# A chunked linear-attention scan with a list scheduler: decays scanned in place, smaller holdings for v and y's decays, other numbers of buffers, and an offset per kind of step

## The chip, the cores and the metric

One core of a Trainium2 chip. The metric is the device time of the whole kernel in microseconds, median over runs. PE is TensorE (PEld its weight loads), DVE VectorE, ACT ScalarE, POOL GpSimd, SP the engine that issues nearly all DMAs.

## The reference

A recurrence over 768 tokens for 4 batches of 8 heads with a 40x40 state each, and then a mixture of 8 experts over the 3072 rows that come out.

```python
for t in range(S):
    y[:, :, t] = np.einsum('bhd,bhde->bhe', rt, state)
    Sa = np.einsum('bhde,bhe->bhd', state, at)
    state_decay = state * wt[:, :, None, :] - np.einsum('bhd,bhe->bhde', Sa, bt)
    state = state_decay + np.einsum('bhd,bhe->bhde', vt, kt)
...
logits = x @ w_gate
expert_idx = np.argmax(logits, axis=1)
...
h = np.maximum(np.einsum('ecd,edf->ecf', disp, w1), 0.0)
y = np.einsum('ecf,efd->ecd', h, w2)
```

Each token goes to one expert, up to a capacity of 768, and is scaled by its softmax gate.

## The kernel before

**Tiling of the scan.** The four batches form two pairs (`pr`), two batches side by side on the 128 partitions. The tokens go in six blocks (`i`) of 128, each of two chunks (`c`) of 64. A block of a pair is numbered n = 2i + pr. The work of one n:

- `decay` (lines 349 to 372): two loads of w, one for products forward from the middle of a group, one backward. DVE scans them (`forth`, `back`) against the tile `seed`, which holds a one at the start of each group, into E and K, the halves of tile R. There are two R, one for each pair. `over`, `divide` and `ends` bring them to one reference point and give the decay of whole chunks, `wf`.
- `prep`: kb (b and k) and a are multiplied by K and E (lines 426, 430). On PE, `xt` (447) forms the 64x64 token products of a chunk in the PSUM tile pd. `take_k` masks one part into an X tile, `xt_inv` (469 and a helper) copies the other into `xd` and `x21`. `kt` and `et` (475) transpose kb into `bk` and E into `EE`, and four DMAs bring `EE` into a tile E, which `take_y` reads.
- `inverse`, once in a block for both pairs and both chunks: the inverse of the unit triangular 32x32 parts, in all partitions at once. `begin` (542) transposes `xd` on DVE, `elim` (556, 558) makes 31 steps of a product and a sum, 62 instructions, each of which reads the one before, `back_a` and `back_b` (563, 567) transpose back. `diag` and `comb` (587) put 64x64 inverses together in the tiles `nt`, by PE and ACT.
- `chain`, for each chunk in order, because it carries the state ST: `enter` (636) decays it, `state` (641) transposes it, `zz` (657, 661) multiplies X by u and the state by a, `take_z` (674) adds the two, `sa` (685) applies `nt`, `turn_sa` and `take_sa` put the result beside v in the tile u, `snew` (720) and `take_snew` (728, 730) give the next state. `out`: `qpm` (739), a mask, `ymm` (754, 760), `take_y` (772). `gate`: y as two fp16 parts, transposed by a DMA, and stored; the router's logits (841).

After each block, `route` counts the tokens of each expert on DVE and PE, and four scatters on POOL's queue (1094) write the block's list. The last block's stretch also holds `prefetch` (the first expert's weights, through the tile `wt`, which is one of the two w tiles) and `first_expert`. The expert stage, from a second scheduler with buffers of its own, follows.

A mask (`masked`, line 56 on) has two forms. On DVE it is one product with the tile `mask` (67). Otherwise ACT copies the tile and POOL clears half of it with two affine selects (61, 64).

**What sets the order.** `steps(name)` collects steps with durations by engine, e.g. `"V.71|A.6 G1.4"` for a mask: DVE, or ACT and then POOL. `order` is a list scheduler: it repeatedly takes, of all steps whose `needs` are given and whose `take` buffers are free, the one with the lowest start plus `later[name] + mu * plan - o_tail * tail`, where `plan` is a due time. Of a step's forms it takes the one with the least end plus `PRICE` times the engine's time. The instructions are then issued in that order, each engine working through its own in order. A step that frees a buffer gives it to the next in line. `BUFS` gives the number of buffers of each name: four X, four `nt` (a block needs four of each, one for each pair and chunk), four `bk`, one `xd`, `x21`, `xu` and `nu`. `LATER` is empty, so `later` is 0 for all steps.

```python
LATER = {}
BUFS = {"pd": 2, "ps": 4, "w": 2, "a": 4, "r": 2, "sv": 3, "sat": 2, "u": 3, "bk": 4, "E": 3, "EE": 1, "X": 4, "nt": 4, "zv": 2,
...
able.append((t + plus, index[name], name, t, plus))
```

`load` issues the DMAs of kb, a, r, vt (into `sv`) and v (into u, both chunks of an n in one tile).

Of the kernel before, what the change touches and what calls it, by code (L numbers as in the profile page):

```python
# [22 lines left out]
class Schedule:  # L23
# [69 lines left out]
    def order(self, mu):  # L93
# [26 lines left out]
        later = {x: self.later.get(x.rstrip("0123456789"), 0.0) for x in threads}  # L120
# [98 lines left out]
def scan_part(ctx, tc, two, w, kb, a, r, vt, v, wg, xd, lg, ident, up, SX, slot2, route, prefetch, fill, early):  # L219
# [26 lines left out]
    SHAPE = {"w": ([P, H * P], F32), "a": ([P, H, P], F32), "r": ([P, 2, H // 2, P], F32), "sv": ([P, 2, H // 2, 2, C], F32),  # L246
             "sat": ([P, H // 2, 2, C], F32),
             "u": ([P, 2, 2, HD], F32), "bk": ([P, 2, HD], F32), "E": ([P, 2, HD], F32), "EE": ([P, 2, HD], F32), "zv": ([P, HD], F32), "X": ([P, H * C], F32),
# [17 lines left out]
    wt = free_["w"][0]  # L266
# [10 lines left out]
    seed = one.tile([P, NG * C], F32, name="seed")  # L277
# [55 lines left out]
    def decay(T):  # L333
# [40 lines left out]
        for z in range(2):  # L374
            steps(f"load_w{pr}")(lambda z=z: start(z), "L0>1.5", take=["w"], gives=("load_w", n, z))
        add = steps(f"decay{pr}")
        add(forth, "V2.3", needs=[("load_w", n, 0)] + [("R", n - NR)] * (n >= NR), free=["w"])
        add(back, "V2.3", needs=[("load_w", n, 1)])
        add(over, "V.6", free=["w"])
# [4 lines left out]
    def load(T):  # L384
# [9 lines left out]
        def fetch(name, x):  # L394
            y = T[name] = get(name)
            if name == "u":

                for z in range(2):
                    dma(y[half(z), :, 1 - z], x[pr, i, half(z)].rearrange("p (c n) -> p c n", c=2))
            else:  # L400
                dma(y.rearrange("p h t -> p (h t)") if name == "a" else y.rearrange("p x j t -> p (x j t)"), x[pr, i])
# [15 lines left out]
    def prep(T, G):  # L417
# [1158 lines left out]
```

## Time and profile before

| | |
|---|---|
| median of 3 runs | 825.42 us (825.19 to 826.05) |
| profiled execution, its own time | 818.57 us |
| its span on the core | 816.8 us |
| mean granted PE clock | 0.798 |
| busy PE, PEld | 590.3 us (72%), 468.9 us (57%) |
| busy DVE, ACT, POOL | 496.6 us (61%), 284.8 us (35%), 226.8 us (28%) |

The span runs from the first instruction to the last. Busy times of different engines overlap. The clock is that of PE in shares of 2.4 GHz. An engine's share over the whole span mixes the scan with the expert stage, so the rows below give windows as well.

### The profile page before, as it was taken

Reading aid. Unit: us, or ns where it says so; the run is one execution under the profiler, and the core shown is the slowest. Engines: PE = TensorE matmul, PEld = TensorE weight load, DVE = VectorE, ACT = ScalarE, POOL = GpSimd, SP = SyncE. Lnnn points to the kernel's source line nnn. Section 1 sums busy time; section 2 is a strip of 40 time slices with the busy share of each in tenths; the row PEclk is TensorE's granted clock in tenths of the full one; section 3 lists DMA queues with packets and bytes.
Section 4 is the critical chain, followed back from the end, with each engine's and each line's share of the span. In section 5 each row is a group of like instructions: output and inputs, shape, how many; then the busy total and the mean of one; then the engine's idle time right before and its main releaser. Section 6 shows DMA issues by size and latency. Waiting matters only on the chain. (4 is left out here: it accounts for less than half of the span.)

```text
span 816.8 us, 23980 instructions
## 1 busy us (share of the span) xinstructions
PE 590.3 (72%) x10388; PEld 468.9 (57%) x10388; DVE 496.6 (61%) x979; ACT 284.8 (35%) x615; POOL 226.8 (28%) x302
## 2 busy tenths in 40 slices
PE   0524978287828874797579739968897789799991
PEld 0414868287717764796578639854473445445651
DVE  5899878963996699769973794426331353252320
ACT  0313433352406331534154425424422344143320
POOL 4201342131302431243123202422353143243110
PEclk9975667576965987588659965789998899899996
DMA  8922573356623664455433325476749674665200
GB/s 297 334 69 60 164 229 115 101 103 115 224 98 89 121 213 140 76 116 174 145 71 71 93 82 106 86 158 180 199 75 231 145 162 144 176 167 155 65 10 19
DMA packets 105970, 109.78 MB, mean 134 GB/s; under 512 B 70360, under 2 KB 88282, under 8 KB 105856
## 3 DMA queue, kind: packets, MB, share of 16 engines
q1 hardware_dynamic: 97856, 92.67, 44.2%
q0 software_dynamic: 4256, 9.99, 4.2%
q10 hardware_dynamic: 3744, 5.51, 2.5%
q8 instruction: 83, 1.36, 0.7%
q14 instruction: 31, 0.25, 0.1%
HBM read 83.60 MB, written 10.94 MB: 116 GB/s over the span
## 5 line engine op out<-in xcount | busy, mean ns | idle before, releaser
L1261 PE MATMUL ps<-w,hh 128*128 128x320 f16 (+1 forms) x672 | 101.5, 311 | 15.7 <-ACT hh L1395 12.5
L1398 DVE SCALAR_TENSOR_TENSOR hh<-ps,hh 128x480 f16<-128x480 f32 (+2 forms) x72 | 37.3, 559 | 111.8 <-ACT hh L1395 111.8
L1261 PEld LDWEIGHTS <-hh 128*128 128x128 f16 (+1 forms) x696 | 71.8, 106 | 47.6 <-ACT hh L1395 14.5
L587 PE MATMUL ps<-nu,x 32*32 32x32 f32 x768 | 21.7, 236 | 99.6 <-DVE nu L567 99.6
L1388 PE MATMUL ps<-xT,w 128*128 128x480 f16 (+1 forms) x448 | 84.8, 352 | 5.3 <-DMA xT<-xt 5.3
L587 PEld LDWEIGHTS ps<-nu,x 32*32 32x32 f32 x768 | 21.1, 151 | 100.8 <-ACT nt L56 56.7
L1388 PEld LDWEIGHTS <-w 128*128 128x128 f16 (+1 forms) x512 | 43.4, 98 | 59.3 <-issue 20.5
L556 DVE TENSOR_TENSOR xd<-xu,nu 128x31 f32<-128x31 f32 (+15 forms) x186 | 70.4, 378 | 6.5
L558 DVE TENSOR_TENSOR nu<-nu,xd 128x31 f32<-128x31 f32 (+15 forms) x186 | 70.3, 378 | 6.4
L739 PE MATMUL pd<-r,sv 64*128 64x64 f32 x768 | 65.1, 335 | 8.2 <-DVE xd L469 8.2
L739 PEld LDWEIGHTS pd<-r,sv 64*128 64x128 f32 x768 | 61.6, 242 | 11.7 <-DVE xd L469 9.7
L1181 DVE SCALAR_TENSOR_TENSOR w<-s,w 128x640 f16<-128x640 f32 (+1 forms) x49 | 47.0, 992 | 32.2 <-ACT w L1180 32.2
L754 PE MATMUL ps<-bk,qp 128*64 128x64 f32 (+1 forms) x768 | 57.9, 256 | 9.2 <-POOL qp L64 9.2
L1265 POOL DMA_INDIRECT out_dram<-ob,ri x26 | 25.8, 991 | 130.1 <-ACT ob L1414 111.3
L636 POOL TENSOR_TENSOR ST<-ST,wf 128x320 f32<-128x320 f32 x17 | 14.9, 886 | 155.8 <-DVE ST L730 109.8
L760 PE MATMUL ps<-S,r 128*64 128x64 f32 (+1 forms) x704 | 54.7, 257 | 3.5 <-issue 3.5
L1180 ACT ACTIVATE w<-s 128x640 f16<-128x640 f32 (+1 forms) x49 | 40.5, 876 | 43.9 <-DMA s<-in_moe_w_dram 43.7
L754 PEld LDWEIGHTS ps<-bk,qp 128*64 128x64 f32 x768 | 47.1, 168 | 12.0 <-POOL qp L64 10.1
L1094 POOL DMA_INDIRECT meta<-mt,sloti x24 | 27.5, 1145 | 78.6 <-DVE mt L1091 73.2
L760 PEld LDWEIGHTS ps<-S,r 128*64 128x64 f32 x704 | 45.6, 171 | 3.9 <-issue 3.9
L1395 ACT ACTIVATE hh<-ps 128x480 f16<-128x480 f32 (+2 forms) x72 | 31.7, 494 | 38.1 <-PE ps L1388 25.0
L64 POOL TENSOR_SCALAR_AFFINE_SELECT qp<-qp 64x512 f32<-64x512 f32 x42 | 28.4, 677 | 53.9 <-ACT qp L61 45.1
(182 smaller groups left out, 1220.4 us busy)
## 6 DMA issues: line engine op xcount, KB each, us to landing
w<-in_w_dram SPq DMA_DIRECT2D x24, 512.0 KB, 5.1
slot<-in_kb_dram SPq DMA_DIRECT2D x24, 512.0 KB, 5.6
sv<-in_vt_dram SPq DMA_DIRECT2D x24, 512.0 KB, 3.3
s<-in_moe_w_dram SPq DMA_DIRECT2D x14, 512.0 KB, 5.0
a<-in_a_dram SPq DMA_DIRECT2D x12, 512.0 KB, 6.4
r<-in_r_dram SPq DMA_DIRECT2D x12, 512.0 KB, 3.8
s<-in_moe_w_dram SPq DMA_DIRECT2D x16, 320.0 KB, 5.3
xd<-x SPq DMA_DIRECT2D x24, 192.0 KB, 3.2
```

The lines of the kernel that those rows point to most:

```text
L556: return (lambda: nc.vector.tensor_mul(tv, xu[:, s + 1:, s:s + 1].to_broadcast([P, n, m]), nu[:, s:s + 1, 0:m].to_broadcast([P, n, m])), l ...
L558: lambda: nc.vector.tensor_add(o, o, tv))
L587: nc.tensor.matmul(pa[o, u * 32:(u + 1) * 32], x21[f, uu, :], (n1 if which == 0 else ntd)[f, uu, :], start=True, stop=True)
L739: nc.tensor.matmul(pp[:, h % 2, cols(4 * x + j, C)], T["sv", c][f, x, j].rearrange("p z t -> p (z t)"), T["r"][f, x, j, tok], start=True, ...
L754: nc.tensor.matmul(py[half(x), into(h)], R["qp"][:, h % 2, 4 * x + h // 2, :], T["bk"][c][:, x, wide(h)], start=True, stop=q == 0)
L760: nc.tensor.matmul(py[half(x), into(h)], T["r"][:, x, h // 2, tok], S_[:, lo:lo + (C if h < H - 1 else D)], start=False, stop=True)
L1180: return (lambda: nc.scalar.activation(h, s(), AF.Copy, scale=SW), lambda: nc.vector.scalar_tensor_tensor(l, s(), SW, h, ALU.mult, ALU.sub ...
L1181: lambda: nc.vector.scalar_tensor_tensor(l, s(), SW, h, ALU.mult, ALU.subtract))
L1261: nc.tensor.matmul(po[:, :DM], h[l], rr[:, f, :], start=(f == 0 and m == 0), stop=(f == NF - 1 and m == 2))
L1388: nc.tensor.matmul(s_["h", f + z][:, :n], l, rr, start=m % 7 == 0 and m < 14, stop=m >= 14)
L1395: nc.scalar.activation(s_["hh"][:, 0, f, :n], s_["h", f][:, :n], AF.Relu)
L1398: nc.vector.scalar_tensor_tensor(s_["hh"][:, 1, f, :n], s_["h", f][:, :n], 0.0, s_["hh"][:, 0, f, :n], ALU.max, ALU.subtract)
```

## The change

1. w is loaded into R, and the scans work in place; `over` then stands between the two scans, since it reads w of the backward half (as K) before `back` overwrites it. A load of w waits for R, that is for the muls and `et` of n - 2. The two w tiles are gone; `wt` is a tile of its own, and `seed` is fp16.
2. u and E hold one chunk each: five half-size tiles in place of three whole ones. v is loaded chunk by chunk; a chunk's tile is freed at `snew` (u) or `take_y` (E).
3. Numbers of buffers: X 4 to 7, `nt` 4 to 6, `bk` 4 to 5, `sv` 3 to 2, `zs` 4 to 3.
4. `LATER` holds an offset for each kind of step (a step's name without its digits); `MU` and `PRICE` change. `divide` is always on DVE.

```diff
-    MU = 0.003
-    O_TAIL = 0.0
+    MU = 0.0016
+    O_TAIL = 0
...
-    PRICE = {"V": 1.5, "A": 0.4, "G": 0.2}
+    PRICE = {"V": 3.41, "A": 1.41, "G": 0.14}
...
-    LATER = {}
+    LATER = {"R": 2.12, "chain": 0.019, "comb": -0.079, "decay": 0.178, "diag": -0.044, "early": 2.414,
...
-    BUFS = {"pd": 2, "ps": 4, "w": 2, "a": 4, "r": 2, "sv": 3, "sat": 2, "u": 3, "bk": 4, "E": 3, "EE": 1, "X": 4, "nt": 4, "zv": 2,
-            "xd": 1, "x21": 1, "xu": 1, "nu": 1, "zs": 4, "S": 2, "qp": 2, "y": 2, "x16": 3, "xT": 2}
+    BUFS = {"pd": 2, "ps": 4, "a": 4, "r": 2, "sv": 2, "sat": 2, "u": 5, "bk": 5, "E": 5, "EE": 1, "X": 7, "nt": 6, "zv": 2,
+            "xd": 1, "x21": 1, "xu": 1, "nu": 1, "zs": 3, "S": 2, "qp": 2, "y": 2, "x16": 3, "xT": 2}
...
-    wt = free_["w"][0]
+    wt = two.tile([P, H * P], F32, name="wt")
...
-    seed = one.tile([P, NG * C], F32, name="seed")
+    seed = one.tile([P, NG * C], F16, name="seed")
...
         def forth():
-            nc.vector.tensor_tensor_scan(E, s_[0], seed, 0.0, ALU.mult, ALU.add)
-            put("w", s_[0])
+            nc.vector.tensor_tensor_scan(E, E, seed, 0.0, ALU.mult, ALU.add)
+
+        def over():
+
+            nc.vector.tensor_mul(se[pr], Eg[:, :, M - 1::M], Kg[:, :, M - 2::M])
+            nc.vector.reciprocal(si[pr], se[pr])
 
         def back():
-            nc.vector.tensor_tensor_scan(K[:, ::-1], s_[1][:, ::-1], seed, 0.0, ALU.mult, ALU.add)
...
+            nc.vector.tensor_tensor_scan(K[:, ::-1], K[:, ::-1], seed, 0.0, ALU.mult, ALU.add)
...
+        for z, x in enumerate((E, K)):
+            steps(f"load_w{pr}{z}")(lambda z=z, x=x: dma(x, w[z, pr, i]), "L0>1.5",
+                                    needs=[("R", n - NR)] * (n >= NR), gives=("load_w", n, z))
...
+        def fetch_u(c):
+
+            y = T["u", c] = get("u")
+            for z in range(2):
+                dma(y[half(z), 1 - z], v[pr, i, half(z), c * HD:(c + 1) * HD])
...
-            y = T["E"] = get("E")
-            for x in range(2):
-                for c in range(2):
-                    dma(y[half(x), c, :], T["EE"][half(c), x, :])
+            for c in range(2):
+                y = T["E", c] = get("E")
+                for x in range(2):
+                    dma(y[half(x)], T["EE"][half(c), x, :])
```

The order of the instructions changes on all engines. Two places show it. Line numbers of the changed kernel are two to four above those of before.

DVE, the third elimination (block 2) at its end, in the kernel before; all 62 rows of 556 and 558 stand in this manner, and the chain's `take_snew` (730), `take_y` (772) and `take_z` (674) of block 1 follow:

```order
L556 TENSOR_TENSOR xd_152<-xu_154,nu_155 128x60
L558 TENSOR_TENSOR nu_155<-nu_155,xd_152 128x2x30
L556 TENSOR_TENSOR xd_152<-xu_154,nu_155 128x31
L558 TENSOR_TENSOR nu_155<-nu_155,xd_152 128x31
L563 STREAM_TRANSPOSE xu_154<-nu_155 128x32x32
L567 STREAM_TRANSPOSE nu_155<-xu_154 128x1024
L730 TENSOR_TENSOR ST_208<-ps_115,ST_209 128x8x40
L772 SCALAR_TENSOR_TENSOR y_164<-ps_117,E_140 128x320
L772 SCALAR_TENSOR_TENSOR y_165<-ps_114,E_138 128x320
L674 TENSOR_TENSOR zs_158<-pd_112,zv_150 128x320
```

In the changed kernel the same elimination (560, 562), some rows before its end, with `take_z` (678), a mask of qp (70) and `take_snew` (733) of block 1 in it:

```order
L560 TENSOR_TENSOR xd_159<-xu_161,nu_162 128x252
L562 TENSOR_TENSOR nu_162<-nu_162,xd_159 128x18x14
L678 TENSOR_TENSOR zs_165<-pd_112,zv_158 128x320
L560 TENSOR_TENSOR xd_159<-xu_161,nu_162 128x255
L562 TENSOR_TENSOR nu_162<-nu_162,xd_159 128x17x15
L560 TENSOR_TENSOR xd_159<-xu_161,nu_162 128x256
L562 TENSOR_TENSOR nu_162<-nu_162,xd_159 128x16x16
L70 TENSOR_TENSOR qp_168<-pd_113,mask 128x512
L560 TENSOR_TENSOR xd_159<-xu_161,nu_162 128x255
L733 TENSOR_TENSOR ST_213<-ps_116,ST_214 128x8x40
L562 TENSOR_TENSOR nu_162<-nu_162,xd_159 128x15x17
L560 TENSOR_TENSOR xd_159<-xu_161,nu_162 128x252
```

What stood behind the 62 rows, and more of the chain that had stood ahead of them, now stands between them; `take_y` rows (775) also stand further up and down.

POOL, in the kernel before, around the four scatters of a block's list (1094), in block 2's part of the program; `enter` (636) and two differences of the gate (824, 825) follow them:

```order
L548 AFFINE_SELECT nu_155<-nu_155 128x1024
L1094 DMA meta_70<-mt,sloti 6144x4
L1094 DMA meta_71<-mt,sloti 6144x4
L1094 DMA meta_72<-mt,sloti 6144x4
L1094 DMA meta_73<-mt,sloti 6144x4
L636 TENSOR_TENSOR ST_207<-ST_207,wf 128x8x40
L636 TENSOR_TENSOR ST_209<-ST_209,wf 128x8x40
L824 TENSOR_TENSOR x_0_166<-y_164,x_0_166 128x320
L825 TENSOR_TENSOR x_0_166<-y_164,x_0_166 128x64
```

In the changed kernel, with what each waits for (DMASW are the semaphores of POOL's own DMAs, here of the scatters; line 67 is a mask's affine select, 640 `enter`):

```order
L640 TENSOR_TENSOR ST_214<-ST_214,wf 128x8x40 [waits DVE_49,Pool_49]
L67 AFFINE_SELECT X_146<-X_146 64x512 [waits Activation_49]
L67 AFFINE_SELECT X_146<-X_146 64x512 [waits Pool_49]
L1096 DMA meta_70<-mt,sloti 6144x4 [waits DVE_49,Pool_49]
L1096 DMA meta_71<-mt,sloti 6144x4
L1096 DMA meta_72<-mt,sloti 6144x4
L67 AFFINE_SELECT qp_168<-qp_168 64x512 [waits Activation_49]
L67 AFFINE_SELECT qp_168<-qp_168 64x512 [waits DMASW6_49,DMASW5_49,DMASW4_49]
L67 AFFINE_SELECT qp_168<-qp_168 64x512 [waits Activation_49]
L67 AFFINE_SELECT qp_168<-qp_168 64x512
L67 AFFINE_SELECT qp_169<-qp_169 64x512 [waits Activation_49]
L67 AFFINE_SELECT qp_169<-qp_169 64x512
```

Three of the four scatters now stand directly ahead of the qp masks, whose second select waits until those three have landed, and masks of X and qp that were DVE's (67 before) are on POOL.

## Rows read from the trace of the kernel before

**Rows 1.** The instructions of line 542 (`begin`): count, durations in ns, first and last start.

```profile
L542 DVE STREAM_TRANSPOSE xu<-xd x6: 1943/1966/1980, 43.9 to 458.3; 128x1024 f32<-128x1024 f32 x6
```

**Rows 2.** Windows over periods: length, busy us (instructions) by engine, PEclk, DMA share, GB/s.

```profile
43.90:126.20 82.30, 46.51 (x1138) 41.88 (x1138) 69.18 (x126) 28.97 (x67) 21.86 (x16) 0.65 0.44 133
...
126.20:458.30 332.10, 240.22 (x6116) 224.05 (x6116) 252.72 (x535) 122.64 (x292) 86.15 (x103) 0.73 0.48 122
...
298.60:380.70 82.10, 60.80 (x1530) 56.86 (x1530) 67.05 (x138) 31.43 (x75) 23.48 (x27) 0.73 0.50 127
...
458.30:546.90 88.60, 66.03 (x1418) 60.85 (x1419) 52.96 (x123) 33.32 (x75) 24.53 (x39) 0.69 0.45 108
```

**Rows 3.** Windows over parts of periods: start, two eliminations, a second part, the expert stage.

```profile
0.00:43.90 43.90, 12.75 (x296) 10.77 (x296) 31.54 (x40) 9.20 (x17) 13.76 (x40) 1.00 0.86 294
...
43.90:72.60 28.70, 3.08 (x72) 2.80 (x72) 26.40 (x67) 2.87 (x8) 0.00 (x0) 0.60 0.15 48
...
298.60:330.00 31.40, 16.94 (x308) 16.06 (x308) 29.20 (x66) 6.72 (x15) 5.37 (x8) 0.67 0.34 114
...
330.00:380.70 50.70, 43.86 (x1222) 40.80 (x1222) 37.85 (x73) 24.71 (x62) 18.11 (x19) 0.77 0.60 135
...
546.90:816.80 269.90, 224.79 (x1422) 131.35 (x1419) 90.17 (x156) 90.70 (x167) 80.51 (x105) 0.93 0.55 133
```

**Rows 4.** Groups, DVE, 298.6 to 380.7: xcount | busy us, mean ns | idle us before <-releasers.

```profile
L556 DVE TENSOR_TENSOR xd<-xu,nu 128x31 f32<-128x31 f32 (+15 forms) x31 | 12.1, 389 | 1.1
...
L426 DVE TENSOR_TENSOR slot<-slot,R 128x1024 f32<-128x1024 f32 x4 | 5.2, 1316 | 0.0
...
L349 DVE TENSOR_TENSOR_SCAN R<-w,seed 128x1024 f32<-128x1024 f32 x2 | 4.6, 2290 | 3.7 <-PE pd L475 3.7
...
L430 DVE TENSOR_TENSOR a<-a,R 128x1024 f32<-128x1024 f32 x2 | 2.7, 1344 | 0.0
...
L67 DVE TENSOR_TENSOR qp<-pd,mask 128x512 f32<-128x512 f32 x4 | 2.6, 685 | 1.1 <-PE pd L739 1.1
...
L67 DVE TENSOR_TENSOR X<-pd,mask 128x512 f32<-128x512 f32 x3 | 2.1, 684 | 0.6 <-PE pd L447 0.6
...
L52 DVE COPY S<-ps 64x320 f32<-64x320 f32 x2 | 1.0, 488 | 2.3 <-PE ps L641 2.3
...
L1123 DVE TENSOR_TENSOR rank<-ps,base 128x32 f32<-128x32 f32 x1 | 0.2, 192 | 2.3 <-PE ps L1117 2.3
```

**Rows 5.** Timeline of DVE in the second elimination: start us, us, instruction.

```profile
129.21 0.57 DVE L556 TENSOR_TENSOR xd<-xu,nu 128x87 f32<-128x87 f32 x1
129.82 0.68 DVE L558 TENSOR_TENSOR nu<-nu,xd 128x87 f32<-128x87 f32 x1
...
153.02 0.25 DVE L556 TENSOR_TENSOR xd<-xu,nu 128x87 f32<-128x87 f32 x1
153.30 0.25 DVE L558 TENSOR_TENSOR nu<-nu,xd 128x87 f32<-128x87 f32 x1
```

**Rows 6.** Groups, POOL, 298.6 to 380.7.

```profile
L64 POOL TENSOR_SCALAR_AFFINE_SELECT qp<-qp 64x512 f32<-64x512 f32 x8 | 5.4, 671 | 10.0 <-ACT qp L61 9.7
```

**Rows 7.** Timeline of POOL, last scatter of a block and the mask behind it.

```profile
181.17 0.97 POOL L1094 DMA_INDIRECT meta<-mt,sloti  x1 [0.30 <-issue]
183.01 0.65 POOL L64 TENSOR_SCALAR_AFFINE_SELECT qp<-qp 64x512 f32<-64x512 f32 x1 [0.87 <-ACT qp L61]
190.81 0.66 POOL L64 TENSOR_SCALAR_AFFINE_SELECT qp<-qp 64x512 f32<-64x512 f32 x1 [7.15 <-DMA meta<-mt,sloti]
```

**Rows 8.** DMA issues: KB each, median us from issue to landing.

```profile
w<-in_w_dram SPq DMA_DIRECT2D x24, 512.0 KB, 5.1
```

**Rows 9.** Windows of 5 us around PE's clock.

```profile
160.00:165.00 5.00, 5.00 (x183) 4.82 (x180) 4.13 (x8) 2.57 (x5) 3.87 (x5) 0.50 0.82 93
...
170.00:175.00 5.00, 4.48 (x170) 3.97 (x164) 4.66 (x12) 4.28 (x11) 0.00 (x0) 1.00 0.57 154
...
180.00:185.00 5.00, 5.00 (x69) 4.78 (x67) 2.91 (x6) 0.58 (x1) 2.49 (x3) 0.50 0.64 44
```

More of the change, by code (lines that the diff above doesn't have):

```diff
@@ L118, in order @@
             tail[x] = own + max([tail[y] for y in after[x]] or [0.0])
-        later = {x: self.later.get(x.rstrip("0123456789"), 0.0) for x in threads}
+        later = {x: self.later.get(x.translate(self.digits), 0.0) for x in threads}
         wire, lanes, order = [], [0.0] * 8, []
@@ L372, in ends @@
             nc.vector.tensor_copy(we[:, pr, i, :], hi[:, :, 1])
-        for z in range(2):
-            steps(f"load_w{pr}")(lambda z=z: start(z), "L0>1.5", take=["w"], gives=("load_w", n, z))
+        for z, x in enumerate((E, K)):
+            steps(f"load_w{pr}{z}")(lambda z=z, x=x: dma(x, w[z, pr, i]), "L0>1.5",
+                                    needs=[("R", n - NR)] * (n >= NR), gives=("load_w", n, z))
         add = steps(f"decay{pr}")
-        add(forth, "V2.3", needs=[("load_w", n, 0)] + [("R", n - NR)] * (n >= NR), free=["w"])
-        add(back, "V2.3", needs=[("load_w", n, 1)])
-        add(over, "V.6", free=["w"])
+        add(forth, "V2.3", needs=[("load_w", n, 0)])
+        add(over, "V.6", needs=[("load_w", n, 1)])
+        add(back, "V2.3")
         for z in range(2):
@@ L395, in fetch @@
             y = T[name] = get(name)
[L396 to L401, printed above, removed]
+            dma(y.rearrange("p h t -> p (h t)") if name == "a" else y.rearrange("p x j t -> p (x j t)"), x[pr, i])
+        def fetch_u(c):
+            y = T["u", c] = get("u")
+            for z in range(2):
+                dma(y[half(z), 1 - z], v[pr, i, half(z), c * HD:(c + 1) * HD])
         def fetch_v(c):
@@ L406, in fetch_v @@
             dma(y.rearrange("p x j z t -> p (x j z t)"), vt[pr, i, c])
-        for name, x, off in (("a", a, 0.0), ("u", v, 20.0), ("r", r, 30.0)):
+        for name, x, off in (("a", a, 0.0), ("r", r, 30.0)):
             PLAN[0] = base + off
-            steps(f"load_{name}{pr}")(lambda name=name, x=x: fetch(name, x), "L0>1.45" if name != "u" else "L0>.6&L0>.6",
-                                      take=[name], gives=("load_" + name, n))
+            steps(f"load_{name}{pr}")(lambda name=name, x=x: fetch(name, x), "L0>1.45", take=[name], gives=("load_" + name, n))
+        for c in range(2):
+            PLAN[0] = base + 20 + 25 * c
+            steps(f"load_u{pr}")(lambda c=c: fetch_u(c), "L0>.3&L0>.3", take=["u"], gives=("load_u", n, c))
         for c in range(2):
@@ L505, in move_e @@
         def move_e():
-            y = T["E"] = get("E")
-            for x in range(2):
-                for c in range(2):
-                    dma(y[half(x), c, :], T["EE"][half(c), x, :])
+            for c in range(2):
+                y = T["E", c] = get("E")
+                for x in range(2):
+                    dma(y[half(x)], T["EE"][half(c), x, :])
             put("EE", T["EE"])
@@ L530, in prep @@
         add(take_et, "A.71|V.8", free=["pd"])
-        add(move_e, "L0>.3&L0>.3&L0>.3&L0>.3", take=["E"], free=["EE"], gives=("E", n))
+        add(move_e, "L0>.3&L0>.3&L0>.3&L0>.3", take=["E", "E"], free=["EE"], gives=("E", n))
         PLAN[0] = base
@@ L656, in zz @@
                     f = half(1 - x)
-                    nc.tensor.matmul(pz[half(x), 1, into(h)], T["X"][c][f, cols(h, C)], T["u"][f, c, x, wide(h)],
+                    nc.tensor.matmul(pz[half(x), 1, into(h)], T["X"][c][f, cols(h, C)], T["u", c][f, x, wide(h)],
                                      start=True, stop=True)
@@ L782, in chain @@
             more(take_state, "A.44&V.5|A.86|V.98", free=["ps"], gives=("Sd", pr, q))
-        add(zz, pe(1.75, 128), needs=[("mula", n), ("take_k", n, c), ("load_u", n)], take=["pd", "zv"] + ["zs"] * (q > 0),
+        add(zz, pe(1.75, 128), needs=[("mula", n), ("take_k", n, c), ("load_u", n, c)], take=["pd", "zv"] + ["zs"] * (q > 0),
             free=["X"] + ["a"] * c)
@@ L794, in chain @@
         if q < NCH - 1:
-            add(snew, pe(1.07, 64), needs=[("bk", n, c)], take=["ps"], free=["u"] * c, gives=("snew", pr, q))
+            add(snew, pe(1.07, 64), needs=[("bk", n, c)], take=["ps"], free=["u"], gives=("snew", pr, q))
             add(take_snew, "V.49", needs=[("state", pr, q - 1)] * (q > 1), free=["ps"])
         else:
-            add(lambda: put("u", T["u"]), "", free=["u"])
+            add(lambda: put("u", T["u", c]), "", free=["u"])
         PLAN[0] += 5
@@ L805, in chain @@
             take=["ps", "y"], free=["qp", "bk"] + ["r"] * c + ["S"] * (q > 0))
-        add(take_y, "V.49", needs=[("E", n)], free=["ps"] + ["E"] * c, gives=("y", pr, q))
+        add(take_y, "V.49", needs=[("E", n)], free=["ps", "E"], gives=("y", pr, q))
         PLAN[0] = base
```

33 lines of the change are left out of this document (14 added, 19 removed).

## The prediction, made before the changed kernel was run

> **What bounds the kernel now.** I read the profile by stretches. In a block of two pairs the tile `xd` is transposed once at the start of a 32-step elimination on DVE (`begin`); that instruction runs six times, first at 43.9 and last at 458.3 us [rows 1], and it cuts the scan into periods. The four from 126.2 to 458.3 take 332.10 us, 83.0 each [rows 2]; the expert stage starts at 546.9 and lasts 269.9 us [rows 3], and no line of the diff touches it.
>
> Each period falls into two parts with different bounds [rows 3]. While the elimination runs (298.6 to 330.0) DVE is busy for 29.20 of 31.40 us, the rest being the gaps between its short steps, and PE for only 16.94. From its end to the next start (330.0 to 380.7) PE is busy for 43.86 of 50.70 us and DVE for 37.85. So the kernel alternates: DVE alone, then mostly PE. Over this period DVE is busy for 67.05 of 82.10 us and PE for 60.80 [rows 2]. The step gaps take 1.1 us for each of the two elimination lines [rows 4], so some 12.9 us of DVE are idle, all in the second part. Rows 4 name their releasers, mostly PE: 3.7 before L349 (the transposes of the decays that held R), 2.3 before the copies of S, 2.3 before `rank`, 1.1 and 0.6 before masks.
>
> The cause is in the rooms. There are four X tiles, which is one block's worth; the next block's last X waits until `zz` of this block's second chunk frees one, and the next elimination waits for that.
>
> **The change part by part.** *Interleaving.* With seven X and six nt tiles the order puts the next elimination beside this block's chain: thirteen or so chain steps (`take_y`, `take_z`, `take_snew`, a mask) now stand between elimination steps on DVE, where 62 stood unbroken. The period can then approach DVE's own work. I add that up from 298.6 to 380.7:
>
> - Busy now 67.05, gaps 2.2.
> - Moved off DVE, by counting the order between two starts: three qp masks (4 to 1), 3 x 0.685 = 2.06; two X masks (3 to 1), 1.37; two copies of S, 0.98 [rows 4]; two casts, two differences and two scalings of nt, less one entry step, about 1.6 by their like. Together 6.0.
> - POOL takes masks as pairs of selects: 58 become 114 over the kernel. They slow the elimination. A step of 128x87 took 0.57 and 0.68 us beside selects and 0.25 without [rows 5]; the first elimination, with POOL idle, needs 26.40 us of DVE, the fourth, with 5.37 us of POOL, 29.20 [rows 3]. That is 0.52 us per us of POOL. The order puts some 14 selects at 0.671 [rows 6], four differences and three entries, about 15 us, beside it: 9.6 more, 5.0 us of DVE.
>
> That makes a floor of 67.05 + 2.2 - 6.0 + 5.0 = 68.3 us. Idle time comes on top. Of the 12.9 some 4 belong to steps that leave DVE; of the rest, part goes since some 30 us of PE's work move beside the elimination. Its bounds are 0 and 12.9; I take 7, nearer the middle since the steps woven in must now find PE finished. So 75.3 against 83.0, 7.7 x 4 = **31 us** less (7 to 59).
>
> *First period, 82.3 us.* DVE is busy 69.18 [rows 2]; 96 instructions stand in it instead of 125. Out go a forward and a backward scan (2.29 each, the backward one taken as the forward), four divisions, two products with kb at 1.316 and three with a at 1.344, three qp masks at 0.685 [rows 4] and six chain takes, about 19 us. 69.2 - 19 + 2.2 of gaps + 2 for POOL's X masks + 6 idle (10.9 before) = 60.4: **22 us** less (15 to 28).
>
> *Start.* All four decay inputs are now loaded first, vt ahead of a and kb, and more decay work stands before the first elimination: 2.3 us more on DVE, after 31.54 of 43.90 [rows 3]. With 8 us idle instead of 12.4 it is 42: **2 us** less (2 more to 5 less).
>
> *Tail.* What is gained by starting the last elimination early is paid in part there: the chain of the block before it now runs beside it. From 458.3 to 546.9 are 88.6 us [rows 2]. Thirteen steps of about 0.49 add 6.4 and POOL 5; PE comes out of the elimination having worked, where it now starts cold: in 160 to 165 us, after its pause, it is granted 0.50 (1.2 GHz) although busy all the time, and 1.00 (2.4 GHz) in 170 to 175 [rows 9]. I credit 3.4 us for that: **8 us** more (2 to 14).
>
> *Decays in place.* w now lands in R itself, so that load waits until the muls and the decay transposes of two pairs ago are done, and on SP stand behind it r, u and vt. A load lands in 5.1 us [rows 8]. Between the release and the scan that reads it the order puts the other pair's decay and muls, over 10 us of DVE, so I cost it at nothing; without that cover it is 5.1 a block. The f16 seed has no row: a scan takes 2.29 us [rows 4], a product of as many elements 1.34; I take 2.29; slower by the 0.95 between the two would cost 4 us a period of four scans, faster by it save 4.
>
> *Halved u and E, sv 3 to 2.* The same bytes in as many or a few more issues; nothing, under PE's and DVE's work.
>
> The sum: 31 + 22 + 2 - 8 = 47 us. The profiled execution took 818.57, so 771.6; the median of the runs shown, 825.42, stands 6.85 above it, which gives **778 us**.
>
> **The rivals.** *DVE almost never waits.* Then the period is 68.3, 28 us better, and the time 750. For it: waiting comes from PE, which is freed for it; against: DVE is in order, and a late PE result now stops the elimination too.
>
> *POOL waits for its own scatters.* Once before, the second select of a mask stood behind four scatters and waited 7.15 us until they landed (183.66 to 190.81) [rows 7]; PE and `take_y` waited with it. In the order that pattern, a wait for landed scatters on a qp select, stands in five blocks. At 7.15 each, beyond my idle time, in four periods: 28.6, so 806. Against: scatters go ahead earlier and land while PE is still at qp.
>
> *The w load is exposed.* One load a block uncovered, 5.1 x 4 = 20: 798.
>
> *The full lock.* If an elimination step stood still for all of a select, 9.6 us of POOL would cost 9.6, not 5.0: 4.6 x 5 = 23, 801. The rows speak for about half: 5.37 us of POOL cost 2.80 [rows 3]. The Trainium skill (SBUF — State Buffer, Who interferes with whom) says that a DVE operation with two SBUF inputs and a GpSimd one that reads SBUF exclude each other, the later one blocked until the first ends; the trace shows the conflict, at half that price.
>
> *Slower: PE at 1.2 GHz throughout.* PE is busy 60.8 us in a period at a mean clock of 0.73 [rows 2]. If its thin work beside the elimination kept it at 0.50, that becomes about 60.8 x 0.73 / 0.50 = 89, the bound of a period: 6 x 4 = 24 worse, the first period only 12 better, the tail 10 worse, start 2 better: 825 + 20 = 845. It beats the forecast once PE's work passes 75 us. For it: 180 to 185, fully busy at 0.50 [rows 9]; against: 170 to 175.
>
> **How the numbers follow.** Forecast 0.52 (762 to 794), DVE never waits 0.14, scatters 0.10, load 0.08, full lock 0.06, slower 0.07, nothing moves 0.03 (gains and waits cancel). The range of 8 in 10 takes the forecast, the load, the lock, and half of the first two rivals: 751 to 812. The measurement tells 0.2% from no change, and faster by more than that gets 0.90, the same 0.03, slower 0.07.
>
> **What would show it.** Right: `begin` at about 42, 102, 177, 253, 328 and 403 us; eliminations of 42 to 46 us with POOL busy for some 15 in them; DVE idle for under 10 us a period; PE's pauses in the elimination gone; the expert stage still about 270 us. Wrong: periods of 80, with DVE's waits on `take_y`, on scans or on PE at 0.50.

## The result and the profile after

The changed kernel takes 781.27 us (median of 4 runs, 774.4 to 785.56) against 825.73 for the kernel before: a ratio of 0.9453, with a 95% interval of 0.9383 to 0.9522. Its profiled execution took 774.4 us with a span of 772.7, against 818.57 and 816.8; so the two spans differ by 44.1 us, the medians by 44.5. The changed kernel's runs lie further apart (1.4%) than those of before (0.2%). Of the experiments below, the profiled executions of e2, e4 and e8 took 1.6%, 2.5% and 0.6% more than their kernels' medians, so their rows are read for where the time goes rather than for how much.

The source row of `begin` (line 546 now) answers to [rows 1]:

```profile
L546 DVE STREAM_TRANSPOSE xu<-xd x6: 1928/1935/1971, 38.0 to 392.5; 128x1024 f32<-128x1024 f32 x6
```

Windows between these starts, to the last `take_y` (487.6) and to the end, answer to [rows 2, 3]; the columns are the same (us; busy PE, PEld, DVE, ACT, POOL; clock of PE, DMA share, GB/s):

```profile
0.00:38.00 38.00, 12.03 (x280) 10.52 (x280) 34.88 (x46) 8.44 (x17) 22.38 (x43) 0.94 0.84 293
38.00:96.00 58.00, 27.48 (x706) 25.80 (x707) 50.51 (x98) 19.14 (x43) 5.59 (x8) 0.63 0.31 95
96.00:165.60 69.60, 54.43 (x1459) 49.07 (x1456) 64.37 (x121) 36.06 (x86) 31.51 (x38) 0.81 0.54 165
165.60:244.50 78.90, 60.22 (x1528) 55.84 (x1528) 60.15 (x125) 36.08 (x85) 30.05 (x40) 0.76 0.58 146
244.50:319.70 75.20, 64.76 (x1554) 59.68 (x1553) 64.03 (x127) 35.97 (x85) 31.24 (x40) 0.73 0.58 153
319.70:392.50 72.80, 59.14 (x1520) 54.00 (x1518) 58.42 (x121) 36.06 (x86) 28.71 (x40) 0.76 0.54 143
392.50:487.60 95.10, 85.58 (x1946) 77.30 (x1944) 55.82 (x124) 45.09 (x103) 36.66 (x53) 0.77 0.54 126
487.60:772.70 285.10, 229.54 (x1418) 133.36 (x1416) 89.56 (x155) 90.22 (x166) 86.02 (x113) 0.90 0.52 127
```

Stage by stage, beside [rows 2, 3] and what was forecast (us, profiled executions):

| stage | before | after | difference | forecast |
|---|---|---|---|---|
| start to the first `begin` | 43.9 | 38.0 | -5.9 | -2 |
| first period | 82.3 | 58.0 | -24.3 | -22 |
| four periods | 332.1 | 296.5 | -35.6 | -31 |
| last `begin` to last `take_y` | 88.6 | 95.1 | +6.5 | +8 |
| expert stage | 269.9 | 285.1 | +15.2 | 0 |
| span | 816.8 | 772.7 | -44.1 | -47 |

The elimination is now long and no longer DVE's alone. One of the four, and what follows it, as windows; compare the 31.40 and 50.70 us of [rows 3], where PE was busy for 16.94 and 43.86:

```profile
244.50:288.50 44.00, 38.83 (x846) 35.79 (x844) 35.90 (x77) 17.80 (x42) 18.57 (x27) 0.80 0.68 168
288.50:319.70 31.20, 25.94 (x708) 23.88 (x709) 28.13 (x51) 18.16 (x44) 12.67 (x14) 0.62 0.44 132
```

Three fifths of PE's work of this period now lie inside the elimination. What DVE waited for in the four periods (us in total, times, longest), and three of its groups there (the two elimination lines and the forward scan):

```profile
DVE y L775 <- PE ps L763: 18.8, 4, 6.7
DVE ST L733 <- PE ps L724: 9.3, 5, 5.2
...
L560 DVE TENSOR_TENSOR xd<-xu,nu 128x31 f32<-128x31 f32 (+15 forms) x124 | 53.8, 434 | 3.5
L562 DVE TENSOR_TENSOR nu<-nu,xd 128x31 f32<-128x31 f32 (+15 forms) x124 | 52.8, 426 | 3.7
L352 DVE TENSOR_TENSOR_SCAN R<-R,seed 128x1024 f32<-128x1024 f32 x7 | 16.6, 2369 | 0.0
```

The waits are on PE's results for the chain, `take_y` ahead of all. What is gone is PE's own pause: it waited for the end of the elimination (PE's line 587, `comb`, now 591) for 60.6 us in the four periods before, and for 5.7 now:

```profile
PE ps L587 <- DVE nu L567: 60.6, 4, 18.1
```

```profile
PE ps L591 <- DVE nu L571: 5.7, 3, 2.5
```

No scan waits for its load of w (0.0 idle ahead of line 352). The longest period, from 165.6, has the longest waits, and POOL's timeline shows where they start (start, us, instruction, idle before it and its releaser); the last two lines are DVE's:

```profile
167.54 0.98 POOL L1096 DMA_INDIRECT meta<-mt,sloti  x1 [0.30 <-issue]
169.05 0.65 POOL L67 TENSOR_SCALAR_AFFINE_SELECT qp<-qp 64x512 f32<-64x512 f32 x1 [0.54 <-ACT qp L64]
173.84 0.66 POOL L67 TENSOR_SCALAR_AFFINE_SELECT qp<-qp 64x512 f32<-64x512 f32 x1 [4.13 <-DMA meta<-mt,sloti]
...
182.98 2.08 POOL L67 TENSOR_SCALAR_AFFINE_SELECT qp<-qp 64x512 f32<-64x512 f32 x3 [5.24 <-DMA meta<-mt,sloti]
...
177.77 0.49 DVE L775 SCALAR_TENSOR_TENSOR y<-ps,E 128x320 f32<-128x320 f32 x1 [5.22 <-PE ps L763]
...
188.37 0.49 DVE L775 SCALAR_TENSOR_TENSOR y<-ps,E 128x320 f32<-128x320 f32 x1 [6.70 <-PE ps L763]
```

The second select of a qp mask waits for the scatters ahead of it, PE's `ymm` needs the mask, `take_y` needs `ymm`, and the elimination stands behind `take_y` on DVE.

In the expert stage the loss has a place too. DVE's timeline of the changed kernel at the last block's routing (the cast of the slots, line 1130, is what the block's scatters need), POOL's first of these scatters, and the same cast and scatter in the kernel before:

```profile
502.15 0.19 DVE L1129 TENSOR_REDUCE slot<-rank 128x4 f32<-128x32 f32 x1
...
511.12 1.23 DVE L1183 SCALAR_TENSOR_TENSOR w<-s,w 128x1024 f16<-128x1024 f32 x1 [8.71 <-ACT w L1182]
512.26 0.16 DVE L1130 CAST sloti<-slot 128x4 int32<-128x4 f32 x1
...
513.21 1.90 POOL L1096 DMA_INDIRECT meta<-mt,sloti  x1 [14.29 <-DVE m L1484]
```

```profile
561.11 0.17 DVE L1128 CAST sloti<-slot 128x4 int32<-128x4 f32 x1
...
562.06 1.03 POOL L1094 DMA_INDIRECT meta<-mt,sloti  x1 [13.47 <-DVE mt L1091]
...
562.24 1.23 DVE L1181 SCALAR_TENSOR_TENSOR w<-s,w 128x1024 f16<-128x1024 f32 x1
```

Before, the scatters started 15.2 us after the last `take_y` (562.06 against 546.9); now 25.6 (513.21 against 487.6), because a cut of expert weights (line 1183), which waits 8.71 us for ACT's half of it, stands ahead of the cast. From these scatters to the end both take about as long, 254.7 and 259.5 us.

### The profile page after: what moved, and what is told of

It reads as the page before. It is cut to its first block, busy times and chain, and to the rows that moved or that the text cites. A ratio compares the mean times of both kernels' runs of the same rounds, so it can differ in the third digit from the quotient of the medians.

```text
span 772.7 us, 24112 instructions
## 1 busy us (share of the span) xinstructions
PE 593.2 (77%) x10388; PEld 465.6 (60%) x10388; DVE 477.7 (62%) x912; ACT 307.1 (40%) x669; POOL 272.2 (35%) x371
## 5 line engine op out<-in xcount | busy, mean ns | idle before, releaser
L1263 PE MATMUL ps<-w,hh 128*128 128x320 f16 (+1 forms) x672 | 106.2, 319 | 29.7 <-ACT hh L1397 24.9
L1263 PEld LDWEIGHTS <-hh 128*128 128x128 f16 (+1 forms) x696 | 73.0, 108 | 65.2 <-ACT hh L1397 28.7
L562 DVE TENSOR_TENSOR nu<-nu,xd 128x31 f32<-128x31 f32 (+15 forms) x186 | 77.5, 417 | 5.7
L560 DVE TENSOR_TENSOR xd<-xu,nu 128x31 f32<-128x31 f32 (+15 forms) x186 | 76.5, 411 | 5.8 <-DVE xu L546 0.5
L67 POOL TENSOR_SCALAR_AFFINE_SELECT qp<-qp 64x512 f32<-64x512 f32 x74 | 51.7, 698 | 68.6 <-ACT qp L64 35.6
L67 POOL TENSOR_SCALAR_AFFINE_SELECT X<-X 64x512 f32<-64x512 f32 x40 | 39.7, 992 | 67.7 <-ACT X L64 66.2
L757 PE MATMUL ps<-bk,qp 128*64 128x64 f32 (+1 forms) x768 | 52.7, 243 | 12.0 <-POOL qp L67 12.0
L763 PE MATMUL ps<-S,r 128*64 128x64 f32 (+1 forms) x704 | 48.6, 241 | 0.0
L826 POOL TENSOR_TENSOR x<-y,x 128x320 f16<-128x320 f32 x24 | 22.9, 954 | 71.9 <-ACT x L55 61.7
L451 PE MATMUL pd<-a,slot 64*64 64x64 f32 x1536 | 36.6, 268 | 12.6 <-DVE xd L473 7.8
L451 PEld LDWEIGHTS pd<-a,slot 64*64 64x64 f32 x1536 | 34.0, 180 | 15.7 <-DVE xd L473 8.8
```

The lines of the kernel that those rows point to most:

```text
L67: self.nc.gpsimd.affine_select(x, x, pattern=[[0, x.shape[1]], [1, C]], compare_op=ALU.is_gt, fill=0.0, base=0, channel_multiplier=-1)
L451: nc.tensor.matmul(pt[half(x if z else 1 - x), z, h * C:(h + 1) * C], kb_, T["a"][half(x), h, tok(c)], start=True, stop=True)
L560: return (lambda: nc.vector.tensor_mul(tv, xu[:, s + 1:, s:s + 1].to_broadcast([P, n, m]), nu[:, s:s + 1, 0:m].to_broadcast([P, n, m])), l ...
L562: lambda: nc.vector.tensor_add(o, o, tv))
L757: nc.tensor.matmul(py[half(x), into(h)], R["qp"][:, h % 2, 4 * x + h // 2, :], T["bk"][c][:, x, wide(h)], start=True, stop=q == 0)
L763: nc.tensor.matmul(py[half(x), into(h)], T["r"][:, x, h // 2, tok], S_[:, lo:lo + (C if h < H - 1 else D)], start=False, stop=True)
```

## The experiments

My theory went in as: the rooms let the chain stand inside the next elimination, and the gain is what stands there. Times of one set of runs are compared with the kernel before on the same chip, by ratio, since the kernel before did not take the same in each set: 835.7 us in that of the first four, and 822.1 and 821.1 in the other two.

**1. Decays in place and halved holdings alone** (e1):

```diff
-"u": 5, "bk": 5, "E": 5, "X": 7, "nt": 6, "sv": 2, "zs": 3
+"u": 6, "bk": 4, "E": 6, "X": 4, "nt": 4, "sv": 3, "zs": 4
-    MU = 0.0016;  PRICE = {"V": 3.41, "A": 1.41, "G": 0.14};  LATER = {...}
+    MU = 0.003;   PRICE = {"V": 1.5, "A": 0.4, "G": 0.2};     LATER = {}
```

> The changed kernel with parts 3 and 4 of the change undone: w scanned in place, and u and E as chunk halves (six of each, the same bytes as before), but X 4, nt 4, bk 4, zs 4, sv 3, no offsets, MU 0.003 and the old prices. Between the first and last step of an elimination only 1 or 2 other DVE instructions stand, as before. My theory (in-place loads are hidden under the other pair's decay, halves cost nothing): 819 to 829 us, the same as before (825.7). Rival, the load of w is exposed once it must wait for R: about 5.1 us in each of four to five blocks, 841 to 851. Rival, the gain comes from the loads and halves themselves (two tiles less to wait for): below 805.

Measured: 827.87 us, ratio 0.9918 (0.9871 to 0.9964). That is 0.8% faster than before, about what was expected; there is no sign of an exposed load, which would be a ratio of about 1.02 or more.

**2. Rooms undone** (e2): `"X": 7, "nt": 6` back to 4 and 4; `sv` and `zs` stay at their smaller numbers.

> The changed kernel with only X back from 7 to 4 and nt from 6 to 4; offsets, prices and all else kept. Only 4 foreign DVE instructions now stand inside the eliminations 2 to 5 (12, 13, 12, 10 in the changed kernel). My theory (the rooms let the next elimination stand beside the chain, and that is the gain): most of the gain goes, periods of 80 to 83 us between begins instead of 74, 803 to 820 us. Rival, the offsets alone give the gain by a better order: 776 to 790.

Measured: 850.41 us, ratio 1.02 (1.0097 to 1.0303). More than the whole gain goes: the offsets with the old rooms are slower than before. My range was too mild, and the rival is out. PE's pause for the elimination is largely back:

```profile
PE ps L591 <- DVE nu L571: 42.8, 4, 11.3
```

**3. Offsets and prices undone, rooms kept** (e3): the second half of e1's diff alone.

> The changed kernel with all offsets 0, MU 0.003 and the old prices, but the new rooms (X 7, nt 6, bk 5). 4 or 5 foreign DVE instructions stand inside an elimination. My theory (the period falls with what stands inside the elimination, rooms being only the condition): about a third of the gain, 800 to 815 us, with POOL beside the eliminations for about 5 us as before. Rival, rooms alone are enough since they let the elimination start early: 776 to 792.

Measured: 828.39 us, ratio 0.9912 (0.987 to 0.9954), the same as without the rooms. Neither the rival nor my third of the gain came. By stages this nothing is a gain and a loss. The second `begin` comes at 100.3 us, where it was 126.2 before and is 96.0 in the changed kernel (e1: 110.8). The four periods then take 353.3 us, where they took 332.1 and 296.5 (e1: 356.6); the kernel before took 1.2% longer in this set, which is not enough for that. Each is one execution. The four periods, PE's pause and DVE's wait at `take_snew` (728):

```profile
100.30:453.60 353.30, 271.55 (x6062) 245.52 (x6063) 259.82 (x524) 134.07 (x318) 112.02 (x117) 0.69 0.45 126
...
PE ps L586 <- DVE nu L566: 19.7, 4, 6.4
...
DVE ST L728 <- PE ps L719: 8.9, 5, 3.4
```

PE's pause is down to a third, yet PE is busy for 271.55 us at a mean clock of 0.69, with about as many instructions as before (240.22 us at 0.73 [rows 2]). Whether that clock is a cause of the longer periods or comes of them is not shown.

**4. Offsets undone, prices and rooms kept** (e4): `LATER = {}`.

> The changed kernel with all offsets 0, and the new rooms, MU and prices kept. 9 or 10 foreign DVE instructions stand inside the eliminations 2 to 6. My theory (what stands inside the elimination decides): most of the gain stays, 784 to 797 us. Rival, the offsets decide which steps stand where (scatters ahead of masks, takes early enough): 800 us or more.

Measured: 827.78 us, ratio 0.9866 (0.9816 to 0.9915). Nine or ten instructions stand in the elimination, and there is hardly a gain: the theory that their number decides fell here. DVE's waits in the four periods of this kernel (103.7 to 462.7 us; line 728 is `take_snew`), and the window over them:

```profile
DVE ST L728 <- PE ps L719: 44.1, 15, 8.3
DVE qp L70 <- PE pd L737: 21.6, 5, 6.5
```

```profile
103.70:462.70 359.00, 263.98 (x6085) 240.19 (x6085) 246.44 (x501) 140.23 (x329) 123.46 (x154) 0.69 0.46 126
```

DVE does the same work as in the changed kernel (246.44 us against 246.97), yet waits 44.1 us at `take_snew`, with the other steps of the next block queued behind it:

```profile
374.30 0.17 DVE L367 COPY we<-se 128x8 f32<-128x8 f32 x1
381.70 0.49 DVE L728 TENSOR_TENSOR ST<-ps,ST 128x320 f32<-128x320 f32 x1 [7.24 <-PE ps L719]
382.35 0.48 DVE L468 SCALAR_TENSOR_TENSOR xd<-pd,mhi,xd 128x256 f32<-128x256 f32 x1 [0.15 <-ACT x L59]
```

So the second theory: the offsets put the block's preparation (decays, products with K and E) ahead of the chain's takes, which then find PE done. It rests on this one execution: in e3, also without offsets, the wait at `take_snew` was 8.9 us.

**5. The changed kernel again** (e5), as a control for the next three.

> The changed kernel itself, beside the runs that follow, on the same chip. Theory: the ratio to before is the one already measured, 0.938 to 0.952, so about 785 to 798 us where before takes 836. Rival, that the gain hangs on the chip (its clock): the ratio comes out above 0.96.

Measured: 774.93 us, ratio 0.9447 (0.9391 to 0.9504). The gain came again, on another chip than that of the first four. The four periods of this control, as one window:

```profile
97.20:396.50 299.30, 239.92 (x6047) 219.27 (x6046) 247.66 (x491) 144.25 (x342) 121.16 (x155) 0.76 0.55 150
```

**6. No wait for the scatters** (e6):

```diff
-            for z in range(2):
-                x = out[z * C:(z + 1) * C]
-                self.nc.gpsimd.affine_select(x, x, ...)
+            self.nc.gpsimd.tensor_mul(out, out, m)
```

> The changed kernel with POOL's form of a mask as one product of the copied tile and the mask tile, in place of two selects on its halves; the order of all other instructions is the same. No POOL instruction now waits for the landing of the scatters (in the changed kernel the second select of a pair did, ten times). Theory that these waits are on the path (POOL's qp masks waited 18.5 us for scatters in the four periods, and DVE's take_y 18.8 us behind them): 10 to 19 us less than the control. Rival, the waits are covered or others take their place: within 5 us of the control. Rival, a product with two SBUF operands on POOL stops DVE more than a select does: 5 to 20 us more than the control, with the elimination's steps longer.

Measured: 776.17 us, ratio 0.9494 (0.9433 to 0.9556): no difference that can be told. But inside, two things moved. The window, POOL's groups of the product, and DVE's elimination lines (557, 559) in these four periods; then the elimination lines of the control:

```profile
99.80:393.70 293.90, 240.01 (x6054) 219.94 (x6053) 259.48 (x492) 144.21 (x342) 116.40 (x113) 0.77 0.53 153
...
L65 POOL TENSOR_TENSOR qp<-qp,mask 128x512 f32<-128x512 f32 x28 | 36.5, 1314 | 41.9 <-ACT qp L64 35.9 <-ACT lg L845 5.9
...
L557 DVE TENSOR_TENSOR xd<-xu,nu 128x31 f32<-128x31 f32 (+15 forms) x124 | 58.1, 468 | 3.5
L559 DVE TENSOR_TENSOR nu<-nu,xd 128x31 f32<-128x31 f32 (+15 forms) x124 | 56.1, 452 | 3.7
```

```profile
L560 DVE TENSOR_TENSOR xd<-xu,nu 128x31 f32<-128x31 f32 (+15 forms) x124 | 54.9, 443 | 3.5
L562 DVE TENSOR_TENSOR nu<-nu,xd 128x31 f32<-128x31 f32 (+15 forms) x124 | 51.4, 414 | 3.7
```

The qp masks no longer wait for scatters (16.8 us in four waits in the control), and DVE's waits at `take_y` fall from 16.1 to 6.1 us. In return DVE is busy for 11.8 us more (259.48 against 247.66), 7.9 of it in the elimination (114.2 against 106.3), beside products that read two tiles where a select reads one. The four periods are 5.4 us shorter, while two executions of the changed kernel differed by 2.8 (296.5 and 299.3). How much of the one was paid for by the other can't be told from this run; selects without the wait were not tried.

**7. Old prices, the rest kept** (e7).

> The changed kernel with only the prices back (V 1.5, A 0.4, G 0.2); offsets and rooms kept. 34 selects stay on POOL of 114, 40 masks go back to DVE (0.685 us each, some 27 us in all, about 4 in a period); 18, 16, 18, 13 and 14 foreign DVE instructions stand inside the eliminations. Theory (DVE's own work and its conflict with POOL set the period; half a us of DVE per us of POOL): 4 us of masks more and about 4 us of conflict less in a period, so within 8 us of the control. Rival, the waits of masks on POOL (scatters, ACT's copy) matter more than DVE's work: 8 to 20 us less than the control. Rival, the order's fit to these offsets matters most and is lost: 15 us or more above the control.

Measured: 774.11 us, ratio 0.9483 (0.9394 to 0.9572): within 8 us of the control, as by the theory. DVE's work in the four periods rises from 247.66 to 253.87 us only, since its elimination lines fall from 106.3 to 95.6 us when POOL is busy for 78.67 us instead of 121.16:

```profile
94.30:391.20 296.90, 230.28 (x6271) 212.09 (x6267) 253.87 (x523) 131.06 (x316) 78.67 (x93) 0.82 0.58 157
...
L560 DVE TENSOR_TENSOR xd<-xu,nu 128x31 f32<-128x31 f32 (+15 forms) x124 | 50.2, 405 | 3.3
L562 DVE TENSOR_TENSOR nu<-nu,xd 128x31 f32<-128x31 f32 (+15 forms) x124 | 45.4, 366 | 3.3
```

So between these two ways of dealing the masks there is nothing to choose.

**8. The chain's own offsets undone** (e8): `LATER` without chain, state, sat, comb, diag, inverse, decay, out, gate, gate_store, route, unit.

> The changed kernel without the offsets of the chain's own kinds (chain, state, sat, comb, diag, inverse, decay, out, gate, gate_store, route, unit); those of prep (mula, mulk, et, kt, xd, xt, R), of loads and of the early expert are kept. 14, 15, 14, 11 and 13 foreign DVE instructions stand inside the eliminations. Theory (prep ahead of the chain's takes is what the offsets give: without any offsets take_snew waited 44 us for PE in four periods, with decays and muls queued behind it): 0 to 15 us above the control, waits at take_snew under 20 us. Rival, the chain's own offsets place the takes: 25 us or more above the control.

Measured: 776.34 us, ratio 0.9403 (0.9292 to 0.9514): all of the gain stays, with 15.2 us of waits at `take_snew`, as the control has them (15.1). These twelve offsets give nothing that can be told.

**9 and 10. Which engine sets the period: more work for DVE, more for PE** (e9, e10). Both issue instructions twice with the same result:

```diff
-            return (lambda: nc.vector.tensor_mul(tv, ...),
+            def product():
+                for _ in range(1 + s % 2):
+                    nc.vector.tensor_mul(tv, ...)
+            return (product,
```

```diff
         def qpm():
-            for h in range(H):
+            for h in [m for m in range(H) for _ in range(2 - m % 2)]:
```

> The changed kernel with every second product of the elimination issued twice (the same result again): 15 more DVE instructions in each of the six eliminations, some 0.39 us each, 6 us of DVE in a period, 35 us in all; the order is otherwise the same. Theory that DVE's own work still sets the period (the floor of the prediction): 4 to 6 us in each of six, 25 to 36 us above the control (775 in the last comparison). Rival, PE with its clock sets it and DVE has room: under 12 us. Rival, the two alternate and both lie on the path: 12 to 25 us.

> The changed kernel with half of the products of qpm issued twice (the same result again): 16 more matmuls in each of the 24 steps, 0.336 us each, 5.4 us of PE in a period, 32 us in all; the order is otherwise the same. Theory that DVE sets the period and PE waits for it: under 10 us above the control (775 in the last comparison). Rival, PE sets it: 25 to 33 us. Rival, the two alternate and both lie on the path: 10 to 25 us.

Measured: 800.0 us, ratio 0.9734 (0.9641 to 0.9828) for DVE, and 826.75 us, 1.0082 (1.0039 to 1.0126) for PE. Their four periods as windows, DVE's first:

```profile
102.80:418.30 315.50, 250.30 (x6054) 230.05 (x6052) 270.23 (x551) 144.36 (x342) 120.14 (x155) 0.73 0.51 142
```

```profile
97.00:420.30 323.30, 273.12 (x6303) 254.18 (x6302) 244.99 (x491) 144.11 (x342) 121.44 (x155) 0.77 0.50 139
```

Against the control's window (299.30 us, DVE 247.66, PE 239.92), 22.6 us more of DVE made it 16.2 us longer, and 33.2 us more of PE 24.0 longer: 0.72 us per us for both. These are single executions, the control is of the set before, and in e9 PE too was busy for 10.4 us more, at a clock of 0.73 against 0.76, so the 0.72 of DVE is not DVE's alone. Still, work added to either engine made the periods longer by less than itself, as it would if the two alternate on the path. By ratio e9 came out 23.6 us above the control, in the range of that rival (25.1 by the medians, on its edge); e10 came out 52 us above, beyond all three ranges, 18.6 of it behind the last `begin`, where PE was busy for 110.65 of 116.50 us (86.91 of 97.90 in the control). That PE's addition came to 8.3 us a period, not the 5.4 that I had put down, has a reason that the timeline shows: a step of `qpm` in the control, and one with 48 matmuls in place of 32 in e10, both at a granted clock of 1.00,

```profile
279.44 2.05 PE L742 MATMUL pd<-r,sv 64*128 64x64 f32 x32
```

```profile
286.05 3.84 PE L742 MATMUL pd<-r,sv 64*128 64x64 f32 x48
```

take 2.05 and 3.84 us: half as many matmuls again take 1.87 times as long.

**11 and 12. Prep's offsets alone, and all but these** (e11, e12): `LATER` cut to mula, mulk, et, kt, xd, xt and R, and `LATER` without them.

> The changed kernel with only the offsets of prep left (mula -0.397, mulk -0.373, et -0.765, kt 0.072, xd -0.475, xt -0.189, R 2.12), those of the chain, the loads, the route and the early expert all 0. 12, 18, 12, 15 and 15 foreign DVE instructions stand inside the eliminations. Theory (prep ahead of the chain's takes is what the offsets give): ratio to before 0.94 to 0.955, as the control. Rival, the loads' offsets give it (w early, r late), prep's alone are not enough: 0.97 or more, as without any offset (0.987).

> The changed kernel with the offsets of prep 0 (mula, mulk, et, kt, xd, xt, R) and all others kept, the reverse of the run before. 11, 11, 11, 11 and 13 foreign DVE instructions stand inside the eliminations. Theory (prep's offsets give the gain): ratio 0.97 or more, take_snew waiting for PE again, over 30 us in four periods. Rival, the other offsets or the number of instructions inside the elimination suffice: 0.94 to 0.96.

Measured: 790.01 us, ratio 0.9566 (0.9466 to 0.9666) with prep's alone, 801.37 us, 0.9743 (0.9662 to 0.9824) without them. From 0.9866 without any offset, prep's give about three of the four points, the others about one alone; without prep's most is lost. Each of these ratios is good to about a point. That is the theory's side in both for which offsets matter, but not for why: 0.9566 lies just outside the range I gave, though its interval reaches into it, and in the last kernel the waits at `take_snew` were 15.6 us, not above 30, with 16.6 in e11 and 15.1 in the control. The waits of e12 were spread, and PE itself waited for masks:

```profile
DVE y L770 <- PE ps L758: 19.0, 5, 7.5
DVE ST L728 <- PE ps L719: 15.6, 7, 4.7
...
PE ps L838 <- DMA xT<-x: 23.5, 15, 3.3
PE ps L752 <- POOL qp L67: 23.5, 12, 5.9
```

No version beat the changed kernel by more than the measurement can tell.

## Why the prediction came out right, and where its steps did not

*The sum* was 47 us for the profiled execution, 44.1 came; 778 us was forecast, 781.27 measured, in the direction given 0.90. Part of the fit is luck: the expert stage lost 15.2 us that were put at nothing, and the four stages of the scan together came out 12.3 better than forecast. That the median stands 6.9 us above the profiled execution again (781.27 against 774.4) is luck too, since that execution was the lowest of four that lie 11 us apart.

*The cause.* "With seven X and six nt tiles the order puts the next elimination beside this block's chain": right as a condition, since without the rooms the same offsets lose 2% (e2), and PE's pause for the elimination, which was to go, went (60.6 to 5.7 us; 42.8 without the rooms). Not right as the whole cause: the rooms alone, with 4 to 10 instructions inside the elimination, bring nothing in sum beyond the first two parts of the change (e1, e3, e4 all near 0.99). Most of the gain up to the second `begin` comes without any offset (100.3 us in e3, 96.0 in the changed kernel, 126.2 before, 123.4 in e2); what the offsets give is in the four periods, 353.3 against 296.5. The offsets of prep are the largest part of them (e11, e12). By what wait they work is not shown: `take_snew`, the place that my second theory named, waited for 2.1 (e7) to 16.6 us (e11) with them, for 15.6 without them (e12), for 8.9 without any offset (e3), and for 44.1 in e4 alone. I had read from the order that both were at work, and weighed only the rooms.

*The floor.* "The period can then approach DVE's own work." This step failed, though the period came out (74.1 us forecast as 75.3). DVE's work was taken from the one period of [rows 4], 67.05 us; over four periods it was 252.72 / 4 = 63.2 [rows 2]. The change in that work was nearly as costed (-1.0; measured 246.97 / 4 = 61.7, so -1.4). But then DVE's idle time before was 19.8 us a period, not 12.9 and the gaps, and after it is 12.4, not 7 and the gaps. A base too high by 4 and an idle time too low by about the same cancelled, which is luck. And PE is as much the bound as DVE: some 0.7 us of period for each us of either (e9, e10).

*POOL's conflict with the elimination* was put at 0.52 us of DVE for each us of POOL, all of it beside the steps. The rate was right and the share wrong. The four eliminations had 18.0 us of POOL each (the four sum to 72.0), and their two lines take 106.6 us, against 4 x 21.2 for the first elimination (10.6 for each line), beside which POOL does nothing [rows 3], so 0.30 for each us of POOL. Step by step, each step less its own time in the first elimination: 25.8 us of selects beside steps cost DVE 13.0 us, or 0.50; 16.8 us of gate differences and entries cost 8.8, or 0.52; and 147 steps with no POOL instruction beside them cost nothing. But only 45.4 of the 72.0 us fell beside steps. So POOL cost 2.9 us more in a period than before (106.6 against 95.2 in the four), not 5.0. *The full lock* is out: a us of select cost half a us. The Trainium skill (SBUF — State Buffer, Who interferes with whom) calls the ports that DVE and GpSimd share an exclusive lock; the conflict shows here, at half of that price.

*POOL waits for its own scatters.* The waits came, four in the four periods, but of 4.6 us on average (18.5 in all; 16.8 in the control), not 7.15; they lay inside the idle time that remained. Taking them away gave no gain that can be told in e6, where DVE was busy for 11.8 us more beside the products.

*First period* and *start*: -24.3 and -5.9 against -22 and -2; DVE was busy for 34.88 of the first 38.00 us, so hardly idle, where I had left it 8 us.

*Tail*: +6.5 to the last `take_y`, near the 8 forecast; its terms were not tested apart. *Expert stage*: "no line of the diff touches it" was the wrong test. The early steps of the first expert and the fill of weights are dealt by the scan's scheduler, with offsets of their own: +15.2 us, of which 10.4 are the last block's scatters, later behind a weight cut. With other offsets (e11, e12) this stage took 271.5 and 271.8 us, but the tail before it 106.9 and 116.9. From the scatters to the end it is 253.0 and 261.4 there, so the two seem to trade ahead of the scatters.

*Decays in place*: 0, right (e1; 0.0 idle before the scans). *The f16 seed*: 2.37 and 2.30 us a scan against 2.29, right.

*PE at 1.2 GHz throughout*: out; the four periods had clocks of 0.73 to 0.81, where [rows 2] has 0.73 over the four.

*What would show it*: the begins came 4 to 11 us ahead of the list; POOL was busy for 16.8 to 18.6 us in the eliminations (15 said); DVE's idle time was 5 to 19 us a period, not under 10; PE's pauses in the elimination were nearly gone, as said; the expert stage was 285, not 270.

Open: why the four periods are longer without the offsets (e1, e3) than before, and whether PE's clock is the reason; by what wait the offsets of prep work, and which of the seven does it; `MU`, which was never put back with the offsets kept; what selects without the scatter wait would give.

## What to carry to other kernels

Room for two blocks in flight was worth nothing here until the order was tuned for it, above all the place of the next block's preparation, and offsets tuned for wide rooms were a loss with narrow ones: test the two together and each alone, and look at each by stages, since a sum of nothing can hide a gain and a loss. To learn what bounds a period in which two engines are each busy for 80%, issue some of each engine's instructions twice with the same result and divide the added length by the added busy time, with an eye on what the other engine's busy time does; here both gave about 0.7, which a share of busy time does not show. Take an engine's base work from all the periods that the sum multiplies by, and check whether the stage that "isn't touched" is ordered by the same scheduler. Multiply a price of contention by the time that really falls side by side, not by all of the other engine's work.

## What the runs showed of the hardware

Half as many matmuls again cost 87% more time in `qpm` at a granted clock of 1.00, which is 2.4 GHz (2.05 to 3.84 us), and 92% more at 0.50 (3.73 to 7.15). The doubled products follow on the same half of the rows, and write the same place again, where the originals alternate between halves after every second product. That matmuls on alternate halves run side by side is my reading of it; no run isolates it.

A POOL product over 128x512 took 1.31 us for a qp mask in e6, and the two selects 2 x 0.68 in the changed kernel; so the product is no dearer on POOL, but DVE's elimination was 7.9 us longer beside it in four periods. Step by step, 28.7 us of products beside elimination steps cost DVE 20.4 us, or 0.71 for each us, where selects cost 0.50.
